# One read-out for two chunks: state-times-r columns for a pair of chunks carried through the first chunk of the pair

## The chip, the cores and the metric

The kernel runs on one core of a Trainium2 chip. The core has five engines, each with its own instruction stream: TensorE (PE in the profile; its weight loads are listed as PEld), VectorE (DVE), ScalarE (ACT), GpSimd (POOL) and SyncE (SP), which only starts transfers. They meet at semaphores. TensorE writes to PSUM, 8 banks of 512 fp32 numbers for each of the 128 partitions; VectorE and ScalarE read PSUM and write SBUF. The metric is the time of one execution on the device in microseconds (us), as the median of several runs.

## What is computed

The kernel runs a recurrent attention with a 40x40 state for each of 32 heads (4 batches, 8 heads) over 768 steps, and then a mixture of experts over its output. Only the first part is touched:

```python
for t in range(S):
    y[:, :, t] = np.einsum('bhd,bhde->bhe', rt, state)
    Sa = np.einsum('bhde,bhe->bhd', state, at)
    state_decay = state * wt[:, :, None, :] - np.einsum('bhd,bhe->bhde', Sa, bt)
    state = state_decay + np.einsum('bhd,bhe->bhde', vt, kt)
```

The second part picks one of 8 experts for each of the 3072 rows (or none), computes a two-layer network with it, scales by a gate and adds the row.

## The kernel before

**Chunks.** The 768 steps are cut into 24 chunks of 32 steps. Within a chunk the recurrence is solved with matrix products; between chunks the state of each head is handed on. The 32 heads are kept as two halves x = 0 and x = 1 of 16 heads each, and each half has its own buffers. Two neighbouring chunks, 2h and 2h+1, form a pair: the decay products, the scaled k and b (`KB`), a times decay (`L1`) and the transposed right side (`L2`) are made for a pair at a time, so the state has to be rescaled by the decay (`Dx`) only when it passes from one pair to the next.

**The buffer R.** For each half and chunk there is one SBUF buffer `R1[x][c%2]` of 128 partitions by 16 heads by 72 columns. Its 128 rows are of four kinds: 40 of the state (`eo`), 32 of the chunk's v (`ao`), 32 of the solved values (`uo`), and unused ones. Columns 0 to 39 lead to the next state, columns 40 to 71 to the output: there the rows hold state times r (made by `rs`), v times r (made by `m2`) and the solved values that belong to r (made by `uq`).

**What is done for one chunk and half**, each a run of 16 small fp32 matrix products, one for each head, and then copies from PSUM:

- `rs` (line 280): state (`SS`) times r into a PSUM tile of 8x32, then two writes into R's state rows, columns 40 to 71: for an even chunk by DVE with the product with `Dx` (line 292), for an odd one by ACT as a plain copy (line 293).
- `ux` (294): L1 times R, 72 columns a head, one ACT copy to `UXs` (304).
- `uq` (306): the triangular inverse times `UXs`, 72 columns, four ACT copies into R's rows for the solved values (315), then POOL multiplies columns 40 to 71 by a causal mask (317).
- `sst` (318): the new state twice over, as `ST` (325; L2 times R's columns 0 to 39) and, transposed, as `S2` (330). `ST` goes into the next chunk's R, columns 0 to 39, by ACT (335) within a pair and by DVE with `Dx` (334) from pair to pair; `S2` goes to `SS` by ACT (338), from where the next `rs` reads it.
- `yy` (340): R's columns 40 to 71 times L2 gives the output, scaled by DVE (352) and sent to HBM.
- `m2` (200): v times r of the next chunk, four ACT copies into R (209).

r and v of a chunk are loaded together into a tile `rvt` of two buffers (line 104).

**The loop.** Pass c of the loop at line 465 treats chunk c: `rs(c,0)`, `uq(c-1,1)`, `yy(c-1,0)`, `ux(c,0)`, `sst(c-1,1)`, `m2(c+1,0)`, `uq(c,0)`, `rs(c,1)`, `yy(c-1,1)`, `sst(c,0)`, `ux(c,1)`, `m2(c+1,1)`. The second half thus runs half a pass behind the first. Between these stand pieces of other work, dealt out by hand: the decay scans of a later pair on DVE (lines 114 to 126) and POOL's `kbm` and `l1a` in even passes, the transposes `kbt` and their 16 ACT copies (188) in odd passes, the steps of a triangular inverse on DVE (`T()`, lines 228 and 230), and the routing of finished rows to experts (`RP`).

**What sets the order.** PE, ACT and DVE run in the order in which the calls are written (line 888); nothing overtakes on them. The order of POOL's instructions and of the transfers in the loop is made by the language's planner from the dependences. PSUM tiles come from rings: `ps_c` (two banks, for `rs`, `ux`, `uq`), `ps_s` (two, for `sst`), `ps_p` (two), and one each for the output and for the inverse. Who takes a ring's tile waits until its last content has been read.

Of the kernel before, what the change touches and what calls it, by code (L numbers as in the profile page):

```python
# [57 lines left out]
def attn(ctx,tc,i,m,out,X):  # L58
# [42 lines left out]
    rvt={}  # L101
    def load_rv(c,E=G):
        if c>=NC: return
        rvt[c]=wk2.tile([128,2,16,32],F32,tag="rvt",name="rvt"); E.dma_start(rvt[c],i['rv'][c])
    def load_v(c,x):
        if c>=NC: return
        SP.dma_start(R1[x][c%NR1][ao[x]:ao[x]+32,:,0:40],i['vt'][c,x])
# [91 lines left out]
        A.copy(wt,pt.rearrange("p h (x e) -> p h x e",x=2)[:,:,:,0:40])  # L199
    def m2(c,x):  # L200
        if c>=NC: return
        t=rvt[c]; rr=t[:,0].rearrange("p (b h) t -> p b h t",b=2); vv=t[:,1].rearrange("p (b h) t -> p b h t",b=2)
        Pp=ps_p.tile([128,4,32],F32,tag="pp",name="psP")
        for hh in range(4):
            for b in (0,2,1,3):
                s=slice(64*(b//2),64*(b//2)+40)
                TE.matmul(Pp[32*b:32*b+32,hh,:],vv[s,b%2,2*hh+x,:],rr[s,b%2,2*hh+x,:],start=True,stop=True)  # L207
        for b in range(4):
            A.copy(R1[x][c%NR1][ao[x]:ao[x]+32,4*b:4*b+4,40:72],Pp[32*b:32*b+32])  # L209
    def tinv(ph):  # L210
        ab=AB[0]
        NLt=sq(NL_)
# [65 lines left out]
                (V.tensor_copy,A.copy)[E[b]](TBa[w].rearrange("p (x f c) m -> p c x f m",x=2,c=2)[r,c,:,:,16:32],p[r].rearrange("p (x f) m -> p x f m",x=2))  # L278
        yield s1,s2,full
    def rs(c,x):  # L280
        if c>=NC: return
        cc=c%2; rr=rvt[c][:,0].rearrange("p (b h) t -> p b h t",b=2)
        R=R1[x][c%NR1]; e=slice(eo[x],eo[x]+40)
        RS=ps_c.tile([128,8,32],F32,tag="pc",name="psRS")
        for hh in range(4):
            for b in (0,2,1,3):
                s=slice(64*(b//2),64*(b//2)+40); v=(b%2)*4+hh
                TE.matmul(RS[s,v,:],SS[x][:,b//2,v,:],rr[:,b%2,2*hh+x,:],start=True,stop=True)  # L288
        for bh in range(2):
            s=slice(64*bh,64*bh+40)  # L290
            o=R[e,8*bh:8*bh+8,40:72]
            if cc==0: V.tensor_tensor(o,RS[s],H[c//2]['Dx'][x][s].unsqueeze(2).broadcast_to([40,8,32]),ALU.mult)
            else: A.copy(o,RS[s])
    UXd={}
    def ux(c,x):
        if c>=NC: return
        R=R1[x][c%NR1]; l1=L1[x][(c//2)%NL]
        UX=ps_c.tile([128,4,72],F32,tag="pc",name="psUX")
        for hh in range(4):
            for b in range(4):  # L300
                u=4*b+hh
                TE.matmul(UX[32*b:32*b+32,hh,:],l1[:,u,c%2,:],R[:,u,:],start=True,stop=True)
        UXs=wk2.tile([128,4,72],F32,tag="UX",name="UXs")
        A.copy(UXs,UX)
        UXd[x]=UXs
    def uq(c,x):
        if c<0: return
        R=R1[x][c%NR1]; Tb=TBa[(c//2)%NTB]; uu=slice(uo[x],uo[x]+32)
        UQ=ps_c.tile([128,4,72],F32,tag="pc",name="psUQ")
        for hh in range(4):  # L310
            for b in range(4):
                q=slice(32*b,32*b+32)
                TE.matmul(UQ[q,hh,:],Tb[q,x*8+hh*2+c%2,:],UXd[x][q,hh,:],start=True,stop=True)  # L313
        for b in range(4):
            A.copy(R[uu,4*b:4*b+4,:],UQ[32*b:32*b+32,:,:])  # L315
# [1 line left out]
        (V if c==NC-1 else G).tensor_tensor(R[pq,:,40:72],R[pq,:,40:72],mQ[pq].unsqueeze(1).broadcast_to([64,16,32]),ALU.mult)  # L317
    def sst(c,x):
        if c<0 or c+1>=NC: return
        R=R1[x][c%NR1]; Rn=R1[x][(c+1)%NR1]; l2=L2[x][(c//2)%NL2]; cc=c%2; e=slice(eo[x],eo[x]+40)  # L320
        ST=ps_s.tile([128,8,40],F32,tag="ps",name="psST")
        for hh in range(4):
            for b in (0,2,1,3):
                u=4*b+hh; v=(b%2)*4+hh; s=slice(64*(b//2),64*(b//2)+40)
                TE.matmul(ST[s,v,:],l2[:,cc,u,:],R[:,u,0:40],start=True,stop=True)  # L325
        S2=ps_s.tile([128,8,40],F32,tag="ps",name="psS")
        for hh in range(4):
            for b in (0,2,1,3):
                u=4*b+hh; v=(b%2)*4+hh; s=slice(64*(b//2),64*(b//2)+40)
                TE.matmul(S2[s,v,:],R[:,u,0:40],l2[:,cc,u,:],start=True,stop=True)  # L330
        for bh in range(2):
            s=slice(64*bh,64*bh+40)
            o=Rn[e,8*bh:8*bh+8,0:40]
            if cc==1: V.tensor_tensor(o,ST[s],H[c//2+1]['Dx'][x][s].unsqueeze(2).broadcast_to([40,8,40]),ALU.mult)
            else: A.copy(o,ST[s])
        for bh in range(2):
            s=slice(64*bh,64*bh+40)
            A.copy(SS[x][s,bh],S2[s])  # L338
    Yt={}; XS={}
    def yy(c,x):  # L340
        if c<0: return
        if x==0: Yt[c]=ps_y.tile([128,8,40],F32,tag="py",name="psY")
        Y=Yt[c]
        R=R1[x][c%NR1]; l2=L2[x][(c//2)%NL2]; cc=c%2
        for hh in range(4):
            for b in range(4):
# [1 line left out]
                TE.matmul(Y[32*b:32*b+32,2*hh+x,:],R[:,u,40:72],l2[:,cc,u,:],start=True,stop=True)
# [556 lines left out]
```

## Time and profile before

| | |
|---|---|
| median of 3 runs | 666.92 us (666.47 to 667.1) |
| the profiled execution | 663.83 us |
| its span, first to last instruction | 662.1 us |
| busy: PE, DVE, ACT, POOL | 515.5, 489.7, 419.5, 324.2 us |
| matmul instructions | 14772 |

The span has three stages: a start of about 71 us, in which the first pairs are loaded and prepared, the passes 1 to 23 until about 520 us, and the experts after that. Only the first two are touched. In the profile, an fp32 product appears as two matmul records, so one run of 16 products is 32 records; L288 is line 288. Busy times of an engine in a stretch add up to less than the stretch where the engine waited. The column PEclk is the clock that TensorE was granted, as a share of full speed.

### The profile page before, as it was taken

Reading aid. Unit: us, or ns where it says so; the run is one execution under the profiler, and the core shown is the slowest. Engines: PE = TensorE matmul, PEld = TensorE weight load, DVE = VectorE, ACT = ScalarE, POOL = GpSimd, SP = SyncE. Lnnn points to the kernel's source line nnn. Section 1 sums busy time; section 2 is a strip of 40 time slices with the busy share of each in tenths; the row PEclk is TensorE's granted clock in tenths of the full one; section 3 lists DMA queues with packets and bytes.
Section 4 is the critical chain, followed back from the end, with each engine's and each line's share of the span. In section 5 each row is a group of like instructions: output and inputs, shape, how many; then the busy total and the mean of one; then the engine's idle time right before and its main releaser. Section 6 shows DMA issues by size and latency. Waiting matters only on the chain.

```text
span 662.1 us, 33508 instructions
## 1 busy us (share of the span) xinstructions
PE 515.5 (78%) x14772; PEld 432.2 (65%) x14772; DVE 489.7 (74%) x1182; ACT 419.5 (63%) x1151; POOL 324.2 (49%) x246
## 2 busy tenths in 40 slices
PE   4777776676776787767785877878886899999995
PEld 1543456565664576656664666666775599999995
DVE  7998697858997479973999736864166457888881
ACT  5463674586965778567785677887885354555540
POOL 5481951648545375553946442223132155666661
PEclk8786895799977898878889689988788999999998
DMA  7473665352443525335253333453365266676210
GB/s 227 152 242 107 166 207 160 104 177 63 139 125 107 174 63 150 109 112 168 83 156 88 107 113 81 140 153 113 105 178 167 73 183 201 214 229 216 77 48 24
DMA packets 67446, 91.06 MB, mean 138 GB/s; under 512 B 32564, under 2 KB 54657, under 8 KB 65806
## 3 DMA queue, kind: packets, MB, share of 16 engines
q1 hardware_dynamic: 62350, 74.05, 38.1%
q0 software_dynamic: 4944, 14.80, 6.6%
q8 instruction: 118, 1.93, 1.2%
q14 instruction: 34, 0.28, 0.1%
HBM read 74.03 MB, written 17.08 MB: 138 GB/s over the span
## 4 chain that ended last, share of the span: by engine, by line
PE 24%; DVE 11%; ACT 8%; issue 5%; DMA 2%; POOL 1%; SPq 0%; POOLq 0%; DVEq 0%; ACTq 0%
PE pc L782 5%; PE ps L793 4%; PE px L782 3%; ACT R1t L315 2%; PE py L793 2%; ACT L2t L188 2%; DVE M L228 2%; PE ps L325 2%; DVE ti L789 2%; PE pc L313 1%; PE pc L288 1%; DVE M L230 1%; PE ps L330 1%; ACT SS L338 1%; ACT R1t L209 1%
## 5 line engine op out<-in xcount | busy, mean ns | idle before, releaser
L317 POOL TENSOR_TENSOR R1t<-R1t,mc 64x512 f32<-64x512 f32 x46 | 60.5, 1315 | 104.7 <-ACT R1t L315 72.6
L315 ACT COPY R1t<-pc 32x288 f32<-32x288 f32 x192 | 74.9, 390 | 20.7 <-PE pc L313 17.6
L730 POOL TENSOR_TENSOR WL<-WR,WH 128x1280 fp32r<-128x1280 f32 (+1 forms) x21 | 57.7, 2782 | 8.7 <-ACT WH L729 8.6
L188 ACT COPY L2t<-pq 64x160 f32<-64x160 f32 x184 | 52.8, 287 | 7.5 <-PE pq L185 5.1
L684 POOL DMA_INDIRECT xg<-XS,ix x24 | 25.5, 1064 | 64.3 <-DMA xg<-XS,ix 26.0
L325 PE MATMUL ps<-R1t,L2t 128*40 128x40 f32 x1472 | 48.2, 221 | 11.0 <-issue 5.3
L143 POOL TENSOR_TENSOR WR<-WR,M 128x1024 f32<-128x1024 f32 (+1 forms) x19 | 44.2, 2332 | 25.8 <-DVE M L114 19.7
L228 DVE TENSOR_TENSOR M<-M 128x22 f32<-128x22 f32 (+10 forms) x110 | 55.0, 500 | 0.0
L325 PEld LDWEIGHTS ps<-R1t,L2t 128*40 128x40 f32 x1472 | 39.3, 132 | 18.9 <-ACT R1t L315 8.9
L338 ACT COPY SS<-ps 40x320 f32<-40x320 f32 x92 | 38.7, 420 | 19.9 <-PE ps L330 18.5
L209 ACT COPY R1t<-pq 32x128 f32<-32x128 f32 x184 | 47.2, 256 | 5.5 <-PE pq L207 1.3
L288 PE MATMUL pc<-rvt,SS 128*40 128x32 f32 x1472 | 44.9, 216 | 7.2 <-issue 4.8
L288 PEld LDWEIGHTS pc<-rvt,SS 128*40 128x40 f32 x1472 | 38.3, 135 | 15.4 <-issue 7.8
L330 PE MATMUL ps<-L2t,R1t 128*40 128x40 f32 x1472 | 42.9, 218 | 6.5 <-issue 6.4
L313 PE MATMUL pc<-UXs,TB 32*32 32x72 f32 x1536 | 43.1, 255 | 6.0 <-issue 5.9
L330 PEld LDWEIGHTS ps<-L2t,R1t 128*40 128x40 f32 x1472 | 38.2, 134 | 7.3 <-issue 7.2
L230 DVE TENSOR_TENSOR M<-M 128x22 f32<-128x22 f32 (+10 forms) x110 | 40.8, 371 | 0.0
L230 DVE TENSOR_TENSOR px<-px,M 128x168 f32<-128x168 f32 (+8 forms) x150 | 39.1, 260 | 1.4
L729 ACT CAST WH<-WR 128x1024 fp32r<-128x1024 f32 (+1 forms) x35 | 39.6, 1132 | 0.0
L313 PEld LDWEIGHTS pc<-UXs,TB 32*32 32x32 f32 x1536 | 32.1, 122 | 11.4 <-issue 8.9
L789 DVE CAST ti<-xe 128x2 int32<-128x2 f32 x8 | 39.3, 4911 | 0.2
L174 DVE STREAM_TRANSPOSE M<-pq 128x128 f32<-128x128 f32 x40 | 12.1, 308 | 36.9 <-ACT M L165 24.3
(240 smaller groups left out, 1529.3 us busy)
## 6 DMA issues: line engine op xcount, KB each, us to landing
rvt<-rv POOLq DMA_DIRECT2D x21, 512.0 KB, 3.9
WR<-kb SPq DMA_DIRECT2D x10, 1024.0 KB
WR<-w SPq DMA_DIRECT2D x16, 640.0 KB
WR<-w SPq DMA_DIRECT2D x16, 512.0 KB
M<-wt SPq DMA_DIRECT2D x9, 520.5 KB
M<-at SPq DMA_DIRECT2D x8, 512.0 KB
WR<-w SPq DMA_DIRECT2D x16, 256.0 KB
R1t<-vt SPq DMA_DIRECT2D x48, 80.0 KB
```

The source lines that it names most:

```text
L188: A.copy(L2[x][h%NL2][64-64*x:128-64*x,c,bb*4:bb*4+4,:],pt[64*c:64*c+64,:,64*x:64*x+40])
L209: A.copy(R1[x][c%NR1][ao[x]:ao[x]+32,4*b:4*b+4,40:72],Pp[32*b:32*b+32])
L228: V.tensor_tensor(tv,NLt[:,j,j+1:32].unsqueeze(2).broadcast_to([128,n,k]),X[:,j,lo:hi].unsqueeze(1).broadcast_to([128,n,k]),ALU.mult)
L230: for tv,xv in q: V.tensor_tensor(xv,xv,tv,ALU.subtract)
L288: TE.matmul(RS[s,v,:],SS[x][:,b//2,v,:],rr[:,b%2,2*hh+x,:],start=True,stop=True)
L313: TE.matmul(UQ[q,hh,:],Tb[q,x*8+hh*2+c%2,:],UXd[x][q,hh,:],start=True,stop=True)
L315: A.copy(R[uu,4*b:4*b+4,:],UQ[32*b:32*b+32,:,:])
L317: (V if c==NC-1 else G).tensor_tensor(R[pq,:,40:72],R[pq,:,40:72],mQ[pq].unsqueeze(1).broadcast_to([64,16,32]),ALU.mult)
L325: TE.matmul(ST[s,v,:],l2[:,cc,u,:],R[:,u,0:40],start=True,stop=True)
L330: TE.matmul(S2[s,v,:],R[:,u,0:40],l2[:,cc,u,:],start=True,stop=True)
L730: def low(s,E,o,x,h): E.tensor_tensor(s.R(o),x,h,ALU.subtract)
L782: for n,(a,b) in enumerate(mm): TE.matmul(ph[:,g],R(a),R(b),start=n==0,stop=n==7)
```

## The change

`rs` is called for even chunks only. It multiplies the state at the start of a pair by the r of both chunks, 64 columns: first those of the odd chunk, then those of the even one. R of an even chunk is 104 columns wide: 0 to 39 as before, 40 to 71 for the odd chunk's r, 72 to 103 for its own. `ux`, `uq` and `m2` of an even chunk work on the wider R (104, 104 and 64 columns). The state update of the even chunk then multiplies columns 0 to 71 by L2: that gives the state for the odd chunk and, in the same product, the state rows of the odd chunk's columns 40 to 71. Its result fills two PSUM tiles of 4x72, both banks of `ps_s`, and four ACT copies bring it into the odd chunk's R. `S2` and the copies to `SS` fall away for even chunks; odd chunks update the state as before. POOL's mask is applied to the last 32 columns of R (`n-32:n`) and `yy` reads the last 32.

The load of r is split from that of v: v of a chunk into `vvt`, r of a pair into `rrt`, with the r of the odd chunk in front.

```diff
-    L2t=cp.tile([128,5120],F32,name="L2t"); R1t=cp.tile([128,4608],F32,name="R1t")
+    L2t=cp.tile([128,5120],F32,name="L2t"); R1t=cp.tile([128,5632],F32,name="R1t")
...
-    R1=[[R1t[:,1152*(2*n+x):1152*(2*n+x)+1152].rearrange("p (u n) -> p u n",u=16) for n in range(NR1)] for x in range(2)]
+    R1=[[R1t[:,3328*n+(1664,1152)[n]*x:][:,:(1664,1152)[n]].rearrange("p (u n) -> p u n",u=16) for n in range(NR1)] for x in range(2)]
+    RW=(104,72)
...
-        rvt[c]=wk2.tile([128,2,16,32],F32,tag="rvt",name="rvt"); E.dma_start(rvt[c],i['rv'][c])
+        rvt[c]=wk2.tile([128,16,32],F32,tag="vvt",name="vvt"); E.dma_start(rvt[c],i['vv'][c])
+    rrt={}
+    def load_rr(h,E=G):
+
+        if h>=NH: return
+        rrt[h]=wk2.tile([128,16,64],F32,tag="rrt",name="rrt"); E.dma_start(rrt[h],i['rr'][h])
...
     def m2(c,x):
...
+        n=(64,32)[c%2]
+        rr=rrt[c//2][:,:,0:n].rearrange("p (b h) t -> p b h t",b=2); vv=rvt[c].rearrange("p (b h) t -> p b h t",b=2)
+        Pp=ps_p.tile([128,4,n],F32,tag="pp",name="psP")
...
-            A.copy(R1[x][c%NR1][ao[x]:ao[x]+32,4*b:4*b+4,40:72],Pp[32*b:32*b+32])
+            A.copy(R1[x][c%NR1][ao[x]:ao[x]+32,4*b:4*b+4,40:40+n],Pp[32*b:32*b+32])
...
     def rs(c,x):
-        if c>=NC: return
-        cc=c%2; rr=rvt[c][:,0].rearrange("p (b h) t -> p b h t",b=2)
+
+        if c>=NC or c%2: return
+        rr=rrt[c//2].rearrange("p (b h) t -> p b h t",b=2)
...
-        RS=ps_c.tile([128,8,32],F32,tag="pc",name="psRS")
+        RS=ps_c.tile([128,8,64],F32,tag="pc",name="psRS")
...
-            o=R[e,8*bh:8*bh+8,40:72]
-            if cc==0: V.tensor_tensor(o,RS[s],H[c//2]['Dx'][x][s].unsqueeze(2).broadcast_to([40,8,32]),ALU.mult)
-            else: A.copy(o,RS[s])
+            V.tensor_tensor(R[e,8*bh:8*bh+8,40:104],RS[s],H[c//2]['Dx'][x][s].unsqueeze(2).broadcast_to([40,8,64]),ALU.mult)
...
-        UXs=wk2.tile([128,4,72],F32,tag="UX",name="UXs")
-        A.copy(UXs,UX)
+        UXs=wk2.tile([128,4,104],F32,tag="UX",name="UXs")
+        A.copy(UXs[:,:,0:n],UX)
...
-        (V if c==NC-1 else G).tensor_tensor(R[pq,:,40:72],R[pq,:,40:72],mQ[pq].unsqueeze(1).broadcast_to([64,16,32]),ALU.mult)
+        pq=slice(64-64*x,128-64*x); o=R[pq,:,n-32:n]
+        (V if c==NC-1 else G).tensor_tensor(o,o,mQ[pq].unsqueeze(1).broadcast_to([64,16,32]),ALU.mult)
     def sst(c,x):
...
+        if cc==0:
+            Sb=[ps_s.tile([128,4,72],F32,tag="ps",name="psSb") for _ in range(2)]
+            for hh in range(4):
+                for b in (0,2,1,3):
+                    u=4*b+hh; s=slice(64*(b//2),64*(b//2)+40)
+                    TE.matmul(Sb[b%2][s,hh,:],l2[:,0,u,:],R[:,u,0:72],start=True,stop=True)
+            for b in (0,2,1,3): A.copy(Rn[e,4*b:4*b+4,:],Sb[b%2][64*(b//2):64*(b//2)+40])
+            return
...
-            if cc==1: V.tensor_tensor(o,ST[s],H[c//2+1]['Dx'][x][s].unsqueeze(2).broadcast_to([40,8,40]),ALU.mult)
-            else: A.copy(o,ST[s])
+            V.tensor_tensor(Rn[e,8*bh:8*bh+8,0:40],ST[s],H[c//2+1]['Dx'][x][s].unsqueeze(2).broadcast_to([40,8,40]),ALU.mult)
...
-                TE.matmul(Y[32*b:32*b+32,2*hh+x,:],R[:,u,40:72],l2[:,cc,u,:],start=True,stop=True)
+                TE.matmul(Y[32*b:32*b+32,2*hh+x,:],R[:,u,RW[cc]-32:RW[cc]],l2[:,cc,u,:],start=True,stop=True)
...
-            load_rv(0,SP); load_kb(2)
+            load_rv(0,SP); load_rr(0,SP); load_kb(2)
...
             load_rv(c+2,G if c else SP)
+            if c%2 or c==0: load_rr((c+3)//2,G if c else SP)
```

`ux` and `uq` take n = `RW[c%2]` as their width; their calls are otherwise unchanged.

More of the change, by code (lines that the diff above doesn't have):

```diff
@@ L35, in host @@
     C=np.ascontiguousarray
-    o=dict(wt=wt,at=tl(a,0.),kb=C(np.stack([tl(k,0.),tl(b,0.)],2).reshape(NHP,128,2,16,2,32).transpose(0,1,3,4,2,5)),rv=C(np.stack([tb(r),tb(v)],2)),vt=C(vt),idl=np.stack([ones,up]),zer=np.zeros((128,1152),np.float32))
+    o=dict(wt=wt,at=tl(a,0.),kb=C(np.stack([tl(k,0.),tl(b,0.)],2).reshape(NHP,128,2,16,2,32).transpose(0,1,3,4,2,5)),rr=C(tb(r).reshape(NHP,2,128,16,32)[:,::-1].transpose(0,2,3,1,4).reshape(NHP,128,16,64)),vv=C(tb(v)),vt=C(vt),idl=np.stack([ones,up]),zer=np.zeros((128,1152),np.float32))
     o.update(raw_r=r,raw_k=k,raw_v=v,raw_w=w,raw_a=a,raw_b=b)
@@ L201, in m2 @@
         if c>=NC: return
-        t=rvt[c]; rr=t[:,0].rearrange("p (b h) t -> p b h t",b=2); vv=t[:,1].rearrange("p (b h) t -> p b h t",b=2)
-        Pp=ps_p.tile([128,4,32],F32,tag="pp",name="psP")
+        n=(64,32)[c%2]
+        rr=rrt[c//2][:,:,0:n].rearrange("p (b h) t -> p b h t",b=2); vv=rvt[c].rearrange("p (b h) t -> p b h t",b=2)
+        Pp=ps_p.tile([128,4,n],F32,tag="pp",name="psP")
         for hh in range(4):
@@ L296, in ux @@
         if c>=NC: return
-        R=R1[x][c%NR1]; l1=L1[x][(c//2)%NL]
-        UX=ps_c.tile([128,4,72],F32,tag="pc",name="psUX")
+        R=R1[x][c%NR1]; l1=L1[x][(c//2)%NL]; n=RW[c%2]
+        UX=ps_c.tile([128,4,n],F32,tag="pc",name="psUX")
         for hh in range(4):
@@ L307, in uq @@
         if c<0: return
-        R=R1[x][c%NR1]; Tb=TBa[(c//2)%NTB]; uu=slice(uo[x],uo[x]+32)
-        UQ=ps_c.tile([128,4,72],F32,tag="pc",name="psUQ")
+        R=R1[x][c%NR1]; Tb=TBa[(c//2)%NTB]; uu=slice(uo[x],uo[x]+32); n=RW[c%2]
+        UQ=ps_c.tile([128,4,n],F32,tag="pc",name="psUQ")
         for hh in range(4):
@@ L312, in uq @@
                 q=slice(32*b,32*b+32)
-                TE.matmul(UQ[q,hh,:],Tb[q,x*8+hh*2+c%2,:],UXd[x][q,hh,:],start=True,stop=True)
+                TE.matmul(UQ[q,hh,:],Tb[q,x*8+hh*2+c%2,:],UXd[x][q,hh,0:n],start=True,stop=True)
         for b in range(4):
             A.copy(R[uu,4*b:4*b+4,:],UQ[32*b:32*b+32,:,:])
-        pq=slice(64-64*x,128-64*x)
-        (V if c==NC-1 else G).tensor_tensor(R[pq,:,40:72],R[pq,:,40:72],mQ[pq].unsqueeze(1).broadcast_to([64,16,32]),ALU.mult)
+        pq=slice(64-64*x,128-64*x); o=R[pq,:,n-32:n]
+        (V if c==NC-1 else G).tensor_tensor(o,o,mQ[pq].unsqueeze(1).broadcast_to([64,16,32]),ALU.mult)
     def sst(c,x):
@@ L324, in sst @@
                 u=4*b+hh; v=(b%2)*4+hh; s=slice(64*(b//2),64*(b//2)+40)
-                TE.matmul(ST[s,v,:],l2[:,cc,u,:],R[:,u,0:40],start=True,stop=True)
+                TE.matmul(ST[s,v,:],l2[:,1,u,:],R[:,u,0:40],start=True,stop=True)
         S2=ps_s.tile([128,8,40],F32,tag="ps",name="psS")
@@ L329, in sst @@
                 u=4*b+hh; v=(b%2)*4+hh; s=slice(64*(b//2),64*(b//2)+40)
-                TE.matmul(S2[s,v,:],R[:,u,0:40],l2[:,cc,u,:],start=True,stop=True)
+                TE.matmul(S2[s,v,:],R[:,u,0:40],l2[:,1,u,:],start=True,stop=True)
         for bh in range(2):
             s=slice(64*bh,64*bh+40)
-            o=Rn[e,8*bh:8*bh+8,0:40]
-            if cc==1: V.tensor_tensor(o,ST[s],H[c//2+1]['Dx'][x][s].unsqueeze(2).broadcast_to([40,8,40]),ALU.mult)
-            else: A.copy(o,ST[s])
+            V.tensor_tensor(Rn[e,8*bh:8*bh+8,0:40],ST[s],H[c//2+1]['Dx'][x][s].unsqueeze(2).broadcast_to([40,8,40]),ALU.mult)
         for bh in range(2):
```

## The prediction

> **What bounds the kernel now.** I read the span and the granted clock first, then the busy time of the engines in stretches, one stretch for each pass of the chunk loop; pass c starts with its first burst of line 288. The rows are those of the core, of passes 6 and 7, 12 to 16, and 19 (start:end, length, busy us of each engine, granted clock, share of the DMA engines):
>
> ```profile
> core 0: 662.1 us, clock 0.888
> ...
> core 0: us, PE busy (x) PEld busy (x) DVE busy (x) ACT busy (x) POOL busy (x), PEclk, DMA share, GB/s
> 182.10:206.92 24.82, 15.49 (x616) 12.80 (x607) 23.84 (x75) 12.98 (x39) 13.84 (x13) 0.80 0.42 128
> 206.92:224.14 17.22, 14.08 (x509) 11.70 (x508) 9.45 (x30) 15.23 (x47) 7.50 (x5) 0.90 0.40 113
> 305.95:326.47 20.52, 15.09 (x619) 12.45 (x611) 13.76 (x25) 12.59 (x38) 13.24 (x10) 0.92 0.42 122
> 326.47:345.38 18.91, 16.12 (x513) 13.64 (x512) 18.59 (x62) 16.93 (x54) 10.16 (x9) 0.82 0.44 127
> 345.38:369.67 24.29, 14.56 (x617) 11.67 (x607) 23.75 (x70) 12.99 (x39) 14.86 (x14) 0.89 0.38 114
> 369.67:386.91 17.24, 14.49 (x509) 11.96 (x508) 9.44 (x30) 15.23 (x47) 7.50 (x5) 0.86 0.48 142
> 386.91:404.23 17.32, 14.11 (x620) 11.93 (x611) 5.99 (x20) 11.68 (x35) 6.29 (x7) 0.90 0.30 85
> ...
> 437.39:454.84 17.45, 12.69 (x510) 10.48 (x509) 7.96 (x32) 16.54 (x52) 3.14 (x3) 1.00 0.61 182
> ```
>
> The passes take turns, and that is the key to the case. Passes 6 and 14 have DVE busy 23.84 of 24.82 and 23.75 of 24.29 us: DVE sets them. Pass 13 has DVE at 18.59 of 18.91: DVE again. In passes 7 and 15, the same to two hundredths, DVE is half idle and ACT has 15.23 of 17.2; in pass 19 it has 16.54 of 17.45. So **odd passes end with ACT** (or, one in four, with DVE). In the late even pass 16 ACT has 11.68 of 17.32, DVE 5.99 and PE 14.11. Next the chain of work that ended last, in passes 12, 15 and 16 (start, us, what):
>
> ```profile
> 315.42 0.49 DVE R1t L334
> ...
> 316.17 2.34 DVE M L114
> ...
> 369.74 1.21 PE pc L288 x32
> 370.95 1.16 PE pc L313 x32
> 372.13 0.39 ACT R1t L315
> ...
> 386.98 0.73 PE pc L288 x32
> ...
> 392.24 0.64 PE pc L302 x32
> ...
> 393.32 0.74 PE ps L325 x32
> 394.07 0.61 PE ps L330 x32
> ```
>
> In pass 12 DVE's scans (L114) come right behind the Dx product of the update (L334). Pass 15 opens with two PE bursts, then goes over to ACT; pass 16 runs from burst to burst on PE. So **late even passes end with PE, the middle ones with DVE**. In the waits between 100 and 520 us (who for whom: total, times, longest):
>
> ```profile
> PE pc L302 <- DVE R1t L292: 11.0, 7, 2.9
> POOL rvt L104 <- PE pc L288: 43.1, 12, 7.0
> ```
>
> The first is the even chunk's `ux` waiting for the Dx product that the change doubles. The second is POOL waiting to reload `rvt` until `rs` has read it.
>
> **The change part by part.** The prices, one row for each kind of instruction (count | busy us, mean ns of one | idle before, releaser); the last row is from the view of line 317 alone (ns min/median/max):
>
> ```profile
> L325 PE MATMUL ps<-R1t,L2t 128*40 128x40 f32 x1472 | 48.2, 221 | 11.0 <-issue 5.3 <-ACT R1t L315 4.0
> L330 PE MATMUL ps<-L2t,R1t 128*40 128x40 f32 x1472 | 42.9, 218 | 6.5 <-issue 6.4
> L288 PE MATMUL pc<-rvt,SS 128*40 128x32 f32 x1472 | 44.9, 216 | 7.2 <-issue 4.8 <-ACT SS L338 2.1
> L313 PE MATMUL pc<-UXs,TB 32*32 32x72 f32 x1536 | 43.1, 255 | 6.0 <-issue 5.9
> L348 PE MATMUL py<-L2t,R1t 128*32 128x40 f32 x1536 | 28.3, 219 | 9.2 <-issue 8.6 <-DVE R1t L317 0.6
> L207 PE MATMUL pq<-rvt 40*32 40x32 f32 x1472 | 22.9, 200 | 15.1 <-ACT L2t L188 10.8 <-issue 4.0 <-DMA rvt<-rv 0.3
> L315 ACT COPY R1t<-pc 32x288 f32<-32x288 f32 x192 | 74.9, 390 | 20.7 <-PE pc L313 17.6
> L209 ACT COPY R1t<-pq 32x128 f32<-32x128 f32 x184 | 47.2, 256 | 5.5 <-PE pq L207 1.3 <-POOL R1t L317 1.0 <-issue 0.9
> L338 ACT COPY SS<-ps 40x320 f32<-40x320 f32 x92 | 38.7, 420 | 19.9 <-PE ps L330 18.5
> L293 ACT COPY R1t<-pc 40x256 f32<-40x256 f32 x48 | 17.6, 367 | 4.7 <-PE pc L288 3.9
> L292 DVE TENSOR_TENSOR R1t<-pc,D 40x256 f32<-40x256 f32 x44 | 18.5, 421 | 3.7 <-PE pc L288 2.8
> L104 POOL DMA_DIRECT2D rvt<-rv x21 | 12.8, 612 | 45.3 <-PE pc L288 45.3
> L317 POOL TENSOR_TENSOR R1t<-R1t,mc 64x512 f32<-64x512 f32 x46 | 60.5, 1315 | 104.7 <-ACT R1t L315 72.6 <-issue 22.1 <-DMA xg<-XS,ix 4.9
> ...
> L317 DVE TENSOR_TENSOR R1t<-R1t,mc x2: 682/686/689, 514.4 to 518.9; 64x512 f32<-64x512 f32 x2
> ```
>
> *PE.* A call of 16 products is recorded as 32 matmuls, a burst. Per burst: L288 44.9/46 = 0.98 us, L325 1.05, L330 0.93 (46 bursts each), L313 43.1/48 = 0.90, L348 0.59, L207 22.9/46 = 0.50. Bursts with four column tiles side by side go from 0.59 at 40 columns to 0.90 at 72: +0.31 for 32 more. Those with two side by side have twice the steps, so up to +0.62; but L288 at 32 columns costs what L325 and L330 cost at 40, so part of its widening starts from a floor, and I take +0.5 for `rs` from 32 to 64 (bounds 0 and 0.62). The new update `Sb` (72 columns, two side by side): 0.99 + 0.62 = 1.6 in place of 1.05 + 0.93.
> [...]
> An even pass c now holds: two `rs` +1.0, two `ux` at 104 columns +0.62, one `uq` +0.31, one `sst` −0.38: **+1.55**. An odd pass: two `rs` gone −1.96, two `m2` for the next even chunk at 64 columns +0.62, one `uq` (of the even chunk's second half) +0.31, one `sst` −0.38: **−1.41**. PE in total gains nothing; its work moves from odd to even passes.
>
> *ACT.* (390 − 256)/160 = 0.84 ns for each element more, so 128 more cost 0.107 us. Even pass: four `uq` copies +0.43, two `UXs` +0.21, `sst` four copies of 288 at 0.39 for four of 320 at 0.42, −0.12: **+0.52**. Odd: four L293 copies gone −1.47, eight `m2` copies +0.86, four `uq` copies +0.43, `sst` −0.12: **−0.30**.
>
> *DVE.* No trace row has a 40x512 product from PSUM; L317 on DVE, as long, takes 0.686 (from above, since it has two tensors to read; from below 0.421, no growth). I take 0.686: four a pair, all in the even pass, 4 × 0.265 = **+1.06**.
>
> *The rest.* POOL's mask keeps its 512 columns. The loads carry the same bytes in three tiles for two; one more POOL issue a pair, and the L104 wait of 43.1 us mostly falls away. POOL is busy 7.50 of 17.24 us in pass 15, so neither is on the path: nothing (if that cover went, 0.61 us an issue, one a pair). The first clear of `R1` is a third longer, in a stage that waits for loads: nothing. PSUM rings keep their order: six takings in an even pass, four in an odd one, two tiles.
>
> *The sum.* An even pass gets longer by what its last engine gets. In the DVE-bound ones (as 6 and 14) +1.06. In pass 12's kind PE holds the first half and DVE the second: the first `rs` and `ux` (+0.8) delay the update that releases DVE's scans, and the later product adds 0.5: +1.3. In late ones PE's +1.55 less what its 3.2 idle us take up, +1.2. An odd DVE-bound pass (13): 0. An odd ACT-bound pass: ACT's first long copies start at 372.13, 2.39 after the first `rs` burst; without `rs` they start after the `uq` burst alone, 1.16 plus 0.4 for its width, so 0.8 sooner; from there +0.43 −0.12 +0.43 −0.73, and the last 0.43 of `m2` falls behind the path: about **−0.8**. What is late next is `sst`'s four copies, which cannot start until the whole 1.6 us burst is done.
> Passes 4 to 15, three groups of four: 3 × (1.3 + 0 + 1.06 − 0.8) = +4.7. Passes 16 to 22, four even and three odd: 4 × 1.2 − 3 × 0.8 = +2.4. Pass 23 has a bare path, where `rs`, its copies and `ux` follow each other:
>
> ```profile
> 512.61 1.28 PE L288 MATMUL pc<-rvt,SS 128*40 128x32 f32 x32
> 514.37 0.76 ACT L293 COPY R1t<-pc 40x256 f32<-40x256 f32 x2
> 514.78 1.09 PE L302 MATMUL pc<-R1t,L1t 128*32 128x72 f32 x32 [0.28 <-ACT R1t L293]
> ```
>
> 514.78 − 512.61 = 2.2 go there. Passes 0 to 3: nothing taken. Sum +4.9. The profiled execution took 663.83 us (662.1 of span and 1.7 around it), so 668.7; the median before is 3.1 above that execution, so **672 us** as a median.
>
> **The rivals.**
> *The odd passes give back more (faster).* Place: the start of the odd pass, where the removed burst, its copies and the second half's `rs` all stood ahead of ACT's chain. If the start falls by the whole 1.2 and some of `m2`'s wider copies fit into ACT's remaining gaps, an ACT-bound odd pass (3, 7, 11, 15, 17, 19, 21, 23, with 17 and 21 taken to be as 19) gains 1.6; if the idle 3 us of PE hide most of the wider bursts, an even pass costs 0.6. 11 × 0.6 − 8 × 1.6 = −6.2: **661 us**. It decides from the point where eight odd gains pass eleven even costs, at 1.4 to 1. For it: the opening of 1.21 + 1.16 us in pass 15, and PE idle in every even pass. Against it: DVE in passes 6 and 14 has no gap to hide 1.06 in.
> *Both cancel.* 0.9 each way: 667.
> *The clock (slower).* Bursts of L288 take 1.21 in pass 15 and 0.73 in pass 16, at stretches of lower granted clock (0.80 to 1.00 in the rows above). With 1.41 us less work in an odd pass PE idles more; if one more stretch of four bursts ran low, 4 × 0.48 × 12 = 23: **690 us**.
> *It doesn't do what it says.* If the wide `sst` (columns 0 to 71) came to wait for POOL's mask on the columns beside it, each of the 24 even updates would take L317's 1.3 us on POOL more: 667 + 31 = **698 us**. Against it: L325 reads beside the mask today and its row above names only issue and ACT.
>
> **How the numbers follow.** Forecast (668 to 681) 0.48; odd passes give more 0.30; cancel 0.10; clock 0.06; mask wait or another order of loads 0.06. The measurement can tell about 0.2%, 1.3 us: faster 0.32, same 0.14, slower 0.54. The range 658 to 683 takes in the first rival and PE's full +1.55 in every even pass (11 × 1.55 − 8 × 0.3 ≈ +15); the forecast's own is 668 to 681.
>
> **What would show it.** L288 with 64 columns at 22 bursts, near 1.5 us each; L292 near 0.69; even passes longer by one us, the kind of pass 15 shorter by 0.8 and opening with L313; L315 at two lengths, 0.39 and 0.50. Wrong if even passes keep their length, if passes 6 and 14 show DVE gaps, or if odd ones fall by over 1.5.

## The result and the profile after

| | before | after |
|---|---|---|
| median | 666.03 us (20 runs) | 671.51 us (20 runs) |
| ratio, 95% interval | 1 | **1.0091** (1.0066 to 1.0116) |
| the profiled execution | 663.83 us | 668.49 us |
| mean granted clock, profiled execution | 0.888 | 0.854 |
| busy PE, DVE, ACT | 515.5, 489.7, 419.5 us | 528.8, 489.9, 423.6 us |
| matmul instructions | 14772 | 13236 |

The changed kernel is slower by 0.9%, some 6 us; the forecast was 672 us. The ratio is taken from the fast runs alone (all 20 before, 18 of the 20 after) and is not the quotient of the two medians. The two profiled executions stand 4.66 us apart, the sum had 4.9; but single executions spread over some 9 us before and 12 us after, so a match this close is partly chance. First the span and clock of the changed kernel, then its groups of instructions kept apart by shape (count | busy us, mean ns of one | idle before, releaser). Lines have moved: `rs` is L296 with the product L299 (before L288, L292), `ux` L308 with its copy L310 (L302, L304), `uq` L319 with its copies L321 (L313, L315), the wide update L332 with its copies L333, the odd chunk's update L339 and L344 (L325, L330), `m2` L214 (L207).

```profile
core 0: 666.6 us, clock 0.854
```

```profile
L321 ACT COPY R1t<-pc 32x416 f32<-32x416 f32 x96 | 47.6, 496 | 9.5 <-PE pc L319 7.8
L333 ACT COPY R1t<-ps 40x288 f32<-40x288 f32 x96 | 37.7, 393 | 14.1 <-PE ps L332 12.9
L332 PE MATMUL ps<-R1t,L2t 128*40 128x72 f32 x768 | 36.1, 253 | 2.0 <-issue 1.1 <-ACT R1t L321 0.8
L191 PE MATMUL pq<-mc,WR 104*128 104x104 f32 x184 | 34.9, 328 | 6.3 <-ACT L2t L194 4.9 <-ACT R1t L216 0.9 <-DVE M L180 0.5
L299 DVE TENSOR_TENSOR R1t<-pc,D 40x512 f32<-40x512 f32 x44 | 30.2, 687 | 6.2 <-PE pc L296 5.4
L296 PE MATMUL pc<-rrt,SS 128*40 128x64 f32 x704 | 27.0, 234 | 0.7 <-issue 0.6
```

The single prices came out close. L299 takes 687 ns (taken: 686), the long copy L321 496 (0.39 + 0.107), the copies of the update 393. A burst of L332 is 36.1/24 = 1.50 us (1.6 taken), one of L296 27.0/22 = 1.23 (0.98 + 0.5 taken). L332 names no wait for POOL's mask among its releasers. PE's busy total, which the sum left unchanged, rose by 13.3 us with 10% fewer matmuls. L191 shows one reason: nothing about it was changed, and before it read

```profile
L185 PE MATMUL pq<-mc,WR 104*128 104x104 f32 x184 | 30.0, 293 | 7.9 <-ACT L2t L188 5.2 <-DVE M L174 2.7
```

so the same 184 products cost 4.9 us more. Four of them take 0.52 to 0.58 us where the granted clock is 1.00 and 0.90 to 0.96 where it is 0.50; the timelines show 8 such fours at 0.50 throughout before, and 16 after. To see what widening itself costs, compare whole bursts (32 records) at the length at which each kind is shortest and comes most often, from the PE timelines of before and after (start, length, what); the granted clock is 1.00 in each of those below, and that is meant by full clock:

```profile
375.50 0.81 PE L325 MATMUL ps<-R1t,L2t 128*40 128x40 f32 x32
376.13 0.79 PE L330 MATMUL ps<-L2t,R1t 128*40 128x40 f32 x32
...
385.92 0.46 PE L207 MATMUL pq<-rvt 40*32 40x32 f32 x32 [1.36 <-ACT L2t L188]
386.91 0.81 PE L288 MATMUL pc<-rvt,SS 128*40 128x32 f32 x32
...
395.32 0.70 PE L313 MATMUL pc<-UXs,TB 32*32 32x72 f32 x32
```

```profile
377.96 1.20 PE L332 MATMUL ps<-R1t,L2t 128*40 128x72 f32 x32
379.09 0.65 PE L214 MATMUL pq<-rrt,vvt 40*32 40x64 f32 x32
...
388.85 1.09 PE L296 MATMUL pc<-rrt,SS 128*40 128x64 f32 x32
...
397.70 0.92 PE L319 MATMUL pc<-UXs,TB 32*32 32x104 f32 x32
```

`rs` grew by 0.28 us (0.5 taken), `m2` by 0.19 and `uq` by 0.22 (0.31 taken each), and the wide update costs 1.20 for 0.81 + 0.79 = 1.60, a saving of 0.40 (0.38 taken). The bursts of `ux` go from 0.71 to 0.92 at that clock. At full clock an even pass thus gets 2 × 0.28 + 2 × 0.21 + 0.22 − 0.40 = +0.8 us of PE work, for +1.55 in the sum. The sum's prices were means over all clocks, a fifth to a third above the full-clock lengths (0.98 for 0.81, 1.05 for 0.81, 0.90 for 0.70), so like for like I estimate +1.0.

**Pass by pass.** In the changed kernel odd passes no longer begin with `rs`, so a mark is needed that both kernels have: the start of ACT's copy of the second half's `ux` (L304, L310). A pass below runs from this copy of chunk c−1 to that of chunk c. Passes 12, 14, 15 and 23 by these marks, before and then after (columns as in the windows of the prediction):

```profile
304.92:325.72 20.80, 15.05 (x635) 12.51 (x639) 13.80 (x28) 12.87 (x38) 12.97 (x11) 0.92 0.42 117
...
344.36:366.12 21.76, 13.97 (x629) 11.38 (x631) 21.21 (x55) 12.15 (x37) 14.08 (x12) 0.95 0.38 110
366.12:385.89 19.77, 15.16 (x495) 12.24 (x495) 12.22 (x46) 16.06 (x51) 8.84 (x8) 0.79 0.44 134
...
501.46:515.97 14.51, 9.27 (x394) 7.98 (x390) 6.99 (x23) 8.37 (x24) 3.24 (x3) 0.88 0.49 145
```

```profile
305.67:327.57 21.90, 16.08 (x603) 13.34 (x607) 11.80 (x26) 13.71 (x38) 13.01 (x12) 0.92 0.42 125
...
346.49:369.93 23.44, 16.14 (x595) 13.39 (x599) 22.91 (x56) 12.90 (x37) 14.67 (x13) 0.83 0.37 108
369.93:387.83 17.90, 12.93 (x399) 10.25 (x399) 11.53 (x43) 15.41 (x47) 7.56 (x7) 0.84 0.48 133
...
508.44:518.07 9.63, 7.90 (x296) 6.39 (x293) 3.53 (x18) 7.42 (x21) 3.04 (x3) 0.80 0.58 177
```

Passes 12 and 14 are longer by 1.10 and 1.68, pass 15 is shorter by 1.87, pass 23 by 4.88. All passes, in us:

| stretch | predicted | measured |
|---|---|---|
| up to `ux` of pass 3 | 0 | −1.4 |
| even passes 4 to 22 | +11.9 | +11.6 |
| odd passes 5 to 21 | −4.8 | −3.3 |
| pass 23 | −2.2 | −4.9 |
| from there to the first product of the experts | 0 | +2.8 |
| the rest | 0 | −0.2 |
| sum | +4.9 | +4.7 |

These are sums over one execution of each kernel. In the profiles of nine kernels of the new form below (all but the two that are 5% slower or more), the even passes 4 to 22 come out at +3.0 to +15.5 against before and the odd ones 5 to 21 at −10.0 to −1.4; how near these rows come to the forecast says little.

One line has no counterpart in the sum. Pass 23 gave back twice what was expected, and 2.8 us were lost right behind it. PE's timeline shows where, after and then before:

```profile
515.74 1.43 PE L308 MATMUL pc<-R1t,L1t 128*32 128x72 f32 x32
519.40 0.90 PE L641 MATMUL pq<-mc,XS 128*128 128x128 f32 x3 [2.23 <-DVE XS L673]
520.23 1.18 PE L319 MATMUL pc<-UXs,TB 32*32 32x72 f32 x32
...
533.79 0.39 PE L795 MATMUL px<-xH,WH 128*128 128x256 f32 x1
```

```profile
514.78 1.09 PE L302 MATMUL pc<-R1t,L1t 128*32 128x72 f32 x32 [0.28 <-ACT R1t L293]
515.80 0.55 PE L628 MATMUL pq<-mc,XS 128*128 128x128 f32 x3
516.42 0.70 PE L313 MATMUL pc<-UXs,TB 32*32 32x72 f32 x32
...
528.90 0.39 PE L782 MATMUL px<-xH,WH 128*128 128x256 f32 x1
```

Between the last `ux` and its `uq` stands a routing step (L641, before L628) that reads finished output rows. Before, these rows were there in time. Now that `rs` and its copies no longer stand ahead of `ux`, the routing step waits 2.23 us for DVE, and the last `uq`, which needs nothing of it, stands behind it in PE's order. In the two kernels of the old form (before, and "no odd `rs`" below) the stretch from the last copy of `ux` to the experts' first product is 12.9 and 13.6 us; in eleven of the twelve profiles of the new form it is 15.7 to 18.2, and in the one left, with two filler bursts, 12.4.

Last, the waits between 97 and 520 us (who for whom: total, times, longest):

```profile
PE pc L308 <- DVE R1t L299: 21.5, 17, 4.8
PE ps L339 <- ACT R1t L321: 18.1, 19, 2.2
...
ACT R1t L333 <- PE ps L332: 12.9, 15, 1.9
```

PE waited 11.0 us for the Dx product before and waits 21.5 now. It waits 18.1 us for `uq`'s copies ahead of an odd chunk's update, in a place that cost 4.0 before:

```profile
PE ps L325 <- ACT R1t L315: 4.0, 11, 0.5
```

The four copies of the wide update stand ahead of those copies on ACT, as do the four wider ones of `m2`, and those of the update start only when the whole burst is done. So three theories were to be told apart. **The clock**: with less work in odd passes PE is granted less clock, and that is the loss. **The widths**: the even passes pay for their wider products, above all for Dx on DVE, as the sum had it. **The late copies**: the loss is in how the update's result gets out of PSUM.

### The profile page after: what moved, and what is told of

Its sections match the earlier page's. It is cut to its first block, busy times and chain, and to the rows that moved or that the text cites. A ratio compares the mean times of both kernels' runs of the same rounds, so it can differ in the third digit from the quotient of the medians.

```text
span 666.6 us, 30357 instructions
## 1 busy us (share of the span) xinstructions
PE 528.8 (79%) x13236; PEld 439.1 (66%) x13236; DVE 489.9 (73%) x1182; ACT 423.6 (64%) x1103; POOL 323.1 (48%) x256
## 5 line engine op out<-in xcount | busy, mean ns | idle before, releaser
L321 ACT COPY R1t<-pc 32x416 f32<-32x416 f32 (+1 forms) x192 | 85.0, 443 | 16.2 <-PE pc L319 12.8
L216 ACT COPY R1t<-pq 32x256 f32<-32x256 f32 (+1 forms) x184 | 57.3, 311 | 5.9 <-PE pq L214 1.7
L319 PE MATMUL pc<-UXs,TB 32*32 32x72 f32 (+1 forms) x1536 | 46.7, 263 | 3.8 <-issue 3.0
L333 ACT COPY R1t<-ps 40x288 f32<-40x288 f32 x96 | 37.7, 393 | 14.1 <-PE ps L332 12.9
L339 PE MATMUL ps<-R1t,L2t 128*40 128x40 f32 x704 | 28.6, 240 | 19.7 <-ACT R1t L321 18.1
L319 PEld LDWEIGHTS pc<-UXs,TB 32*32 32x32 f32 x1536 | 34.9, 118 | 12.7 <-issue 8.1
L310 ACT COPY UXs<-pc 128x416 f32<-128x416 f32 (+1 forms) x48 | 21.8, 454 | 33.2 <-PE pc L308 31.9
L191 PE MATMUL pq<-mc,WR 104*128 104x104 f32 x184 | 34.9, 328 | 6.3 <-ACT L2t L194 4.9
L339 PEld LDWEIGHTS ps<-R1t,L2t 128*40 128x40 f32 x704 | 22.9, 149 | 25.1 <-ACT R1t L321 23.0
L235 DVE TENSOR_TENSOR M<-M,px 128x168 f32<-128x168 f32 (+8 forms) x150 | 37.0, 247 | 1.7
L332 PE MATMUL ps<-R1t,L2t 128*40 128x72 f32 x768 | 36.1, 253 | 2.0 <-issue 1.1
L308 PE MATMUL pc<-R1t,L1t 128*32 128x104 f32 (+1 forms) x768 | 26.5, 277 | 13.3 <-DVE R1t L299 12.5
```

The lines of the kernel that those rows point to most:

```text
L216: A.copy(R1[x][c%NR1][ao[x]:ao[x]+32,4*b:4*b+4,40:40+n],Pp[32*b:32*b+32])
L235: V.tensor_tensor(tv,NLt[:,j,j+1:32].unsqueeze(2).broadcast_to([128,n,k]),X[:,j,lo:hi].unsqueeze(1).broadcast_to([128,n,k]),ALU.mult)
L319: TE.matmul(UQ[q,hh,:],Tb[q,x*8+hh*2+c%2,:],UXd[x][q,hh,0:n],start=True,stop=True)
L339: TE.matmul(ST[s,v,:],l2[:,1,u,:],R[:,u,0:40],start=True,stop=True)
```

## The experiments

All ratios are to the kernel before, run beside each kernel on the same chip; its medians there were 664.11 us (runs 1 to 4), 663.46 (5 to 8), 666.61 (9 to 11) and 663.18 (12). The changed kernel itself is at 1.0091. It was not run again beside them, so a difference from it supposes that its ratio is the same on every chip, which no run shows.

**1 and 2. Work put back into the odd passes.** A burst of 16 products of 32 columns into a PSUM tile that nobody reads, where `rs` of the second half stood before; then two of them.

```diff
-            if c: rs(c,1)
+            if c: rs(c,1); fill(c,1,1)
```

> The kernel after the change (671.5 us), and in every odd pass from 3 on, where the second half's rs used to stand, 16 products of the old size (32 columns) into a PSUM tile that nobody reads: work added to PE, none taken away. Theory C (clock): the removed burst leaves PE without work for 2 to 3 us while ACT copies, TensorE's granted clock halves behind that gap, and this eats what the odd passes should have gained; the filler keeps the clock up: 665 to 669 us, and clearly less half-clock time in odd passes than the 93 us of after. Rival W (work): odd passes are not shorter because the wider bursts and copies themselves fill them, the clock is a by-product; 11 more bursts of 0.75 us then cost something: 672 to 679 us, whatever the clock does.

> As the filler run, with two bursts (32 products) in the same place, about 1.5 us of PE work. Theory C: the gap of 2 to 3 us is nearly closed, the half-clock time of odd passes falls to that of before (42 us) or lower and the time is at or below that of one burst, 663 to 668 us. Rival W: another 0.5 to 0.7 us in each of 11 passes, 676 to 686 us.

One burst: 668.04 us, **1.0080** (1.0047 to 1.0112). The mean granted clock of the runs came back from 0.857 to 0.881, where the kernel before has 0.883, and the time hardly moved. So bringing the clock back in this way gains nothing; whether the gain was eaten by the added work (11 bursts near 0.8 us) this run can't tell. Run 7 tells more: there the clock stays at 0.850, and the loss is gone all the same. Two bursts: 696.1 us, 1.0485 (1.0451 to 1.0520), which neither theory expected. The filler's own design did it: the second burst takes the PSUM tile that still holds `uq`'s result, and the wait list of that kernel has a new entry, in which the filler (L308 there) stands behind the copies of `uq` (L330 there):

```profile
PE pc L308 <- ACT R1t L330: 30.1, 11, 3.2
```

It says nothing on the clock.

**3. The Dx product at half its width.** Only the 32 columns of the even chunk's own r are multiplied and written.

```diff
-            V.tensor_tensor(R[e,8*bh:8*bh+8,40:104],RS[s],...broadcast_to([40,8,64]),ALU.mult)
+            V.tensor_tensor(R[e,8*bh:8*bh+8,72:104],RS[s,:,32:64],...broadcast_to([40,8,32]),ALU.mult)
```

> The kernel after the change, with the Dx product on DVE made for the even chunk's own 32 columns only (256 instead of 512 elements; the odd chunk's r columns of the state rows are left at zero). This is the price of the term +1.06 us of DVE in each even pass. My prediction charged it in full in the six DVE-bound even passes of kind 6 and 12 and in part in the others: 664 to 667 us. Rival: the measured even passes grew by only about half a microsecond each, so DVE's longer product is mostly covered: 669 to 672 us.

669.47 us, **1.0087** (1.0053 to 1.0121). The product fell to its old length,

```profile
L299 DVE TENSOR_TENSOR R1t<-pc,D 40x256 f32<-40x256 f32 x44 | 18.5, 420 | 7.0 <-PE pc L296 6.2
```

that is 11.7 us less DVE work in the even passes, and nothing came of it in the whole: −0.04%, with some 0.4% either way. By passes something did. The lengths of the three DVE-bound passes and of the odd passes right behind them, by the marks above, in one execution each (that of run 3, 664.44 us, is its fastest; run 8 narrows this product too):

| passes, together | before | changed | run 3 | run 8 |
|---|---|---|---|---|
| 6, 10, 14 | 65.35 us | 70.83 | 69.18 | 68.94 |
| 7, 11, 15 | 60.20 us | 55.35 | 58.81 | 57.78 |

The short product makes the DVE-bound passes 1.7 to 1.9 us shorter, and the odd passes behind them are 2.4 to 3.5 us longer. What a pass gains is gone by the end of the next one.

**4. The kernel before without the odd `rs` products.** The copies that bring them out stay.

```diff
-        for hh in range(4):
+        for hh in range(4 if cc==0 else 0):
```

> The kernel before the change (666 us) without the matrix products of rs in odd chunks; their tile, its ACT copies and everything else stay (the odd chunks' state part of the output is not computed). It takes 24 bursts of 0.98 us off PE and nothing else. Theory C: PE is not what ends the odd passes, and the gaps cost clock: 664 to 668 us with 20 us or more of additional half-clock time in odd passes. Rival W: work counts, odd passes get 0.5 to 1 us shorter each: 655 to 661 us.

657.98 us, **0.9894** (0.9848 to 0.9939). Taking these bursts away gains 7 us, although the clock falls here too (0.859 as a mean of the runs, against 0.883). As rival W had it, work taken out counts, and that PE idles more does not eat it. (With the products, their copies' wait for them goes too; the run doesn't part the two.) Where the gain arises is less plain. In its profile passes 7, 11 and 15 are 0.9 to 1.2 us shorter each, but the odd passes 5 to 21 together are not (+0.5); the even ones give 5.6 and pass 23 gives 2.5.

**5 to 8. One width taken back at a time**, in the changed kernel: `m2` for the even chunk at 32 columns, `uq` at 72, the wide update at 40 (products and copies), `rs` at 32 (products and Dx).

```diff
-        n=(64,32)[c%2]
+        n=32
...
-            A.copy(R[uu,4*b:4*b+4,:],UQ[32*b:32*b+32,:,:])
+            A.copy(R[uu,4*b:4*b+4,0:72],UQ[32*b:32*b+32,:,:])
...
-            Sb=[ps_s.tile([128,4,72],F32,tag="ps",name="psSb") for _ in range(2)]
+            Sb=[ps_s.tile([128,4,40],F32,tag="ps",name="psSb") for _ in range(2)]
...
-                TE.matmul(RS[s,v,:],SS[x][:,b//2,v,:],rr[:,b%2,2*hh+x,:],start=True,stop=True)
+                TE.matmul(RS[s,v,32:64],SS[x][:,b//2,v,:],rr[:,b%2,2*hh+x,32:64],start=True,stop=True)
```

> The kernel after the change with one widening undone: m2 of an even chunk works on 32 columns instead of 64 (products and four copies; the odd chunk's v-times-r rows in it stay zero). It takes 0.43 us of ACT copies and 0.31 us of PE out of each half of an odd pass. Theory S (the loss is the sum of the widenings, each costing its own work where ACT ends the pass): ratio to before 1.003 to 1.006, that is 2 to 4 us off the 1.0091 of after. Theory O (one widening, the late and wide state update, holds all of the loss): 1.008 to 1.011, no gain.

> The kernel after the change with uq of an even chunk kept at 72 columns (products and four copies; columns 72 to 103 of the solved rows are left as they were). It takes 0.43 us of ACT copies and 0.31 us of PE from each half, half of it in even and half in odd passes. Theory S: 1.003 to 1.006. Theory O: 1.008 to 1.011.

> The kernel after the change with the even chunk's state update at 40 columns instead of 72 (products and four copies of 160 instead of 288 elements; the odd chunk's state part of the output is left out). It takes 0.5 to 0.6 us of PE and 0.4 us of ACT from each half, ahead of the next chunk's ux. Theory S: 1.002 to 1.005. Theory O: it is this update, whose copies start only when the whole burst is done: 0.995 to 1.000.

> The kernel after the change with rs of even chunks at 32 columns, in the products as well as in the Dx product on DVE (the odd chunk's r columns of the state rows stay zero). The narrower Dx product alone gave 1.0087, nothing; so this shows what the wider PE burst costs (0.25 us by its own row, 1.23 against 0.98, in each half of an even pass). Theory S: 1.005 to 1.008. Theory O, or a bound outside PE and DVE in even passes: 1.008 to 1.011.

| taken back | us | ratio, interval | against 1.0091 |
|---|---|---|---|
| `m2` | 668.86 | 1.0056 (1.0021 to 1.0090) | −0.35% |
| `uq` | 668.63 | 1.0082 (1.0052 to 1.0112) | −0.09% |
| update | 661.56 | **0.9967** (0.9940 to 0.9993) | **−1.24%** |
| `rs` | 668.99 | 1.0064 (1.0035 to 1.0093) | −0.27% |

A difference of two such ratios is known to about 0.4%. Only the update stands out of that, and it holds more than the whole loss. By the expectations, `uq` and the update came out where the update alone held the loss, `m2` and `rs` where each widening cost its own work; but these two are within 0.4% of no gain at all. The wider `ux` was not taken back in any run. The mean clock of the narrow update's runs is 0.850, below that of the changed kernel (0.857): the loss goes without the clock coming back.

**9. Products wide, copies narrow.** The update's products stay at 72 columns; ACT copies 40 of them.

```diff
-            for b in (0,2,1,3): A.copy(Rn[e,4*b:4*b+4,:],Sb[b%2][64*(b//2):64*(b//2)+40])
+            for b in (0,2,1,3): A.copy(Rn[e,4*b:4*b+4,0:40],Sb[b%2][64*(b//2):64*(b//2)+40,:,0:40])
```

> The kernel after the change, its wide state update at 72 columns in the products, but the four ACT copies bring only 40 columns (160 instead of 288 elements) into the next R; the odd chunk's state part of the output is left out. With 40 columns in both, the ratio to before was 0.9967 (after: 1.0091), so the update holds 1.2%. Theory A (ACT's copies are what costs: 4 x 0.1 us on the path in each half): 0.996 to 1.001. Theory P (the longer burst on PE, at the end of which the copies start, costs): 1.004 to 1.010.

664.98 us, **0.9973** (0.9946 to 1.0000), −1.18%: the same as with narrow products. Within the 0.4%, it is ACT's part that costs, not PE's:

```profile
L333 ACT COPY R1t<-ps 40x160 f32<-40x160 f32 x96 | 27.5, 287 | 11.4 <-PE ps L332 10.3
```

The copies are 0.106 us shorter each, four in a half: 0.42 us a half, 10.2 us in all, of which 7.9 (1.18% of 666) reach the end. Narrowing `uq` takes as much from ACT (96 copies, 0.106 each) and gains 0.6 us, with 2.7 either way. ACT's time as such is not what counts, but where on ACT it stands.

**10. The same work, its order by banks.** The products that fill the first bank come first, so two of the four copies can start at half of the burst. Nothing is left out.

```diff
-            for hh in range(4):
-                for b in (0,2,1,3):
+            for g in ((0,2),(1,3)):
+                for hh in range(4):
+                    for b in g:
```

> The kernel after the change with the products of the wide update in another order: first all 8 that fill the first bank, then the 8 of the second, so that two of the four copies can start half a burst, some 0.7 us, earlier. Computes the same. Theory P: the lateness of the copies is the cost, 1.000 to 1.005. Theory A: the copies' own time is unchanged, and ACT is busy with other copies meanwhile: 1.007 to 1.011.

667.16 us, **1.0008** (0.9973 to 1.0043), −0.83%. The wait of the copies for the burst goes from 12.9 us to

```profile
ACT R1t L334 <- PE ps L333: 3.9, 9, 1.2
```

9.0 us less between these two profiles; the time falls by 5.5 us (0.83% of 666). Where the first copy waits for its burst, it starts 0.74 us behind the burst's start, for 1.12 in the changed kernel. With the same products and copies, the lateness alone is worth nearly the whole loss; the kernel so ordered is not to be told from the kernel before.

What the runs don't show is the path from these copies to the end of the program. The wait that rose from 4.0 to 18.1 us, of the odd chunk's update for `uq`'s copies, is still there in the runs that gain (17.2 us in run 7, 16.6 in run 9, 16.5 in run 10), so it alone is not where the loss sits.

**11. Both banks as one tile, two copies of 576.**

```diff
-            for b in (0,2,1,3): A.copy(Rn[e,4*b:4*b+4,:],Sb[b%2][64*(b//2):64*(b//2)+40])
+            sv=psS.rearrange("p (b q) -> p b q",b=2)
+            for bh in range(2): A.copy(Rn[e,8*bh:8*bh+8,:]...,sv[64*bh:64*bh+40,:,0:288])
```

> The kernel after the change with both banks of the update cut from one PSUM tile, so that two copies of 576 elements take the place of four of 288. Computes the same. By the slope of the copies (0.84 ns an element, 0.15 us fixed) ACT spends 1.27 instead of 1.57 us in each half. Theory A: 1.002 to 1.006. Theory P: 1.007 to 1.011, since the copies wait for the whole burst as before.

707.6 us, **1.0623** (1.0578 to 1.0669), far from either expectation. The copies did get cheaper (two of 0.633 for four of 0.393), but `ST` and `S2` of the odd chunks now lie in one tile as well, and its wait list begins its ACT part with

```profile
ACT SS L351 <- DVE R1t L348: 40.3, 19, 3.5
```

ACT's copy of `S2` waits until DVE has read `ST`, though these are different banks: 40.3 us in all, and the kernel lost 35 against the changed one (1.0623 − 1.0091 of 666). In the changed kernel, with a tile for each bank, ACT's copy of `S2` waits for PE alone (17.8 us).

**12. Half of the copies on DVE.** The order by banks, and in 8 of the 24 halves (the expectation says 22), where DVE is at most half busy, two of the four copies on DVE.

```diff
+            dv=(c%4==2 and x==1 and c<22) or (c,x) in ((16,0),(20,0),(20,1))
+            for b in (0,2,1,3): (V.tensor_copy if dv and b%2 else A.copy)(...)
```

> The kernel after, with the update's products written bank by bank (as in the run before last) and, in 8 of the 22 halves where DVE is at most half busy (second halves of chunks 2, 6, 10, 14, 18 and the halves of chunks 16 and 20 but one), two of the four copies of the update on DVE in place of ACT. Theory that ACT's copies of the update stand on the path: each of these halves loses two copies of 0.39 us on ACT, 0.8 us at most, of which the order by banks already hides part; 8 x 0.3 to 0.8 = 2.4 to 6.4 us less than the order alone, ratio to the kernel before 0.991 to 0.998. Rival, that what is left is PE's and the late copies were all of it: ACT's shorter chain is not seen, 0.999 to 1.003. Second rival, that DVE, being in order, holds its own next work behind the burst: above 1.004.

672.84 us, **1.0150** (1.0111 to 1.0190): the second rival, and by much. The wait list shows it:

```profile
DVE R1t L335 <- PE ps L333: 31.8, 7, 9.6
```

DVE, which takes its work in the order of the calls, stands up to 9.6 us in front of an update that isn't there yet, and what it would have done meanwhile comes late. That an engine is half idle over a pass doesn't mean that it is free at that point of its order.

**Do the parts add up?** The removed bursts −1.06% (run 4), the update +1.24, `m2` +0.35, `rs` +0.27, `uq` +0.09 (runs 5 to 8): +0.89%, measured +0.91. That nearness is no proof. Each term is known to some 0.4%, so the sum to about 1%; run 4 was made on the other kernel; and three parts of the change were never measured alone: the wider `ux`, the copies L293 that fell away, and `S2` with its copies.

## Why the prediction was right, and where not

**The split by passes came out near, in one execution of each kernel.** Even passes pay, odd ones give back: +11.6 for +11.9 and, with pass 23 and the 2.8 us behind it, −5.4 for −7.0. The scatter between profiles named above is larger than these differences, so part of that is luck. Run 4 shows that the removed bursts are worth 7 us, but its profile doesn't place them in the odd passes. In pass 11 the start of ACT's path moved as worked out. From ACT's timelines before and after (start, length, what):

```profile
288.83 0.53 ACT L630 COPY xT<-pq 128x256 f32<-128x256 f32 x2 [2.23 <-DVE M L228]
290.06 0.75 ACT L293 COPY R1t<-pc 40x256 f32<-40x256 f32 x2 [0.70 <-PE pc L288]
291.19 1.60 ACT L315 COPY R1t<-pc 32x288 f32<-32x288 f32 x4 [0.39 <-PE pc L313]
```

```profile
289.64 0.53 ACT L643 COPY xT<-pq 128x256 f32<-128x256 f32 x2 [0.68 <-PE pq L641]
291.21 2.02 ACT L321 COPY R1t<-pc 32x416 f32<-32x416 f32 x4 [1.04 <-PE pc L319]
```

`uq`'s copies came 2.36 us behind the copy of the transposed output rows (L630), now 1.57 behind it (L643): 0.79 sooner, for the 0.8 taken.

**The price of the widths was too high, and DVE's part of it came to nothing.** The step "in the DVE-bound ones (as 6 and 14) +1.06" took the longer Dx product as what lengthens passes 6, 10 and 14, and added that to the time. They are longer by 1.68, 2.12 and 1.68 us, and with the short product less so; but the odd passes behind them then gave back less, and the time stayed: the term measured 0.3 us, with some 2.8 either way, for 3.2 in the sum. What failed is the adding up, pass by pass, of a length that the next pass takes back. PE's +1.55 was +0.8 at full clock, some +1.0 at the clocks of the sum; the bounds for `rs` (0 and 0.62) held its 0.28, the value taken was too near the upper one. At full clock `rs` grew by 0.28 on 0.81 and `m2` by 0.19 on 0.46, so neither widening was free; between 32 and 40 columns, in `rs` and `ST` before, the length is the same, 0.81 for L288 and L325.

**The term that failed is the update's.** The sum counted `sst` as a saving, −0.38 us on PE and −0.12 on ACT in each pass, and wrote "What is late next is `sst`'s four copies, which cannot start until the whole 1.6 us burst is done" without a price. The savings in busy time are there (1.20 for 1.60 us on PE; four copies of 0.393 for four of 0.42 on ACT), but the start of the copies was put at nothing. Runs 7, 9 and 10 price it: 5.5 us for the lateness, 8 for the update's wide copies as a whole. Before, `ST` filled its tile in a burst of 0.81, and its two copies could run while PE made `S2`; now both tiles are full only at the end of 1.20, and all four copies stand behind that. What dropping `S2` saved against this was not measured alone.

The total is therefore right by luck: as far as these terms are known, the too high price of the widths stood in for the missing price of the late copies. The 672 also began from a median of 666.92 us in three runs; from the 666.03 of 20 runs the same sum gives 671.

**The rivals.** *More given back in odd passes* did happen in pass 23 (−4.9 for −2.2) and in passes 7, 11 and 15 (−1.5, −1.5, −1.9 for −0.8), but 17, 19 and 21 gave −0.3, +0.2 and +0.9. *The clock* fell, as that rival had it, from 0.888 to 0.854 in the profiled executions. In pass 11 it can be watched. From 297.0 to 301.0 PE is busy 1.68 of 4.00 us, as the update L339 waits for ACT, 1.78 and then 0.54 us; the next 3 us run at a granted clock of 0.50. Before the change, at the same place, PE is busy 3.35 of 4.00 us and the clock stays at 1.00. Before and then after:

```profile
296.00:300.00 4.00, 3.35 (x134) 2.60 (x134) 2.50 (x14) 3.79 (x12) 0.91 (x2) 1.00 0.13 25
300.00:303.00 3.00, 2.66 (x98) 2.29 (x98) 0.16 (x2) 2.84 (x10) 1.28 (x1) 1.00 0.62 187
```

```profile
297.00:301.00 4.00, 1.68 (x68) 1.21 (x58) 2.10 (x11) 3.81 (x12) 0.00 (x0) 0.96 0.13 25
301.00:304.00 3.00, 2.95 (x65) 2.72 (x66) 1.07 (x1) 2.21 (x7) 1.28 (x1) 0.50 0.26 75
```

What takes the clock down, no run here shows. The price of 23 us was far off: run 1 brought the clock back for 0.1%, run 7 gained 1.24% at 0.850, and the runs of the order by banks (0.870) and of the narrow copies (0.879), which got faster, changed ACT's work or its start as well. What the clock alone costs stays open. *The mask*: no such wait appeared. *Cancelling*: no.

**What the prediction asked to see.** L296 came with 22 bursts, at 1.23 and not near 1.5; L299 at 0.69; L321 at two lengths, 0.390 and 0.496; passes 6 and 14 showed no new gaps on DVE. Pass 15 opened with L319 and was shorter.

## What to carry to other kernels

When a change makes one burst out of two, price the moment at which its reader can begin, not only the sum of the work: here PE and ACT had less to do in the update, and yet its copies' late start cost 5.5 us. Filling a result bank by bank, so that two of the copies can start at half of the burst, got that back with the same instructions. And don't add up gains pass by pass: what one pass gave in run 3, the next one took. A chain made shorter runs up against whatever stands in the same engine's order for another reason, as the last `uq` did behind the routing step; moving that step is the next thing to try, and wasn't tried.
